# One transformer block's forward and backward on one core: the small vector arithmetic at the turn from forward to backward, regrouped into one set of column sums per norm pair and per gradient pair, with one activation table set

## The chip, the cores and the metric

The kernel runs on one core of one Trainium2 chip. The metric is the device time of one launch in microseconds (us). The kernel before has a median of 1363.42 us in three runs (1362.38 to 1365.44).

## The reference

The reference computes one adaptive-layernorm block on a single token (D = 640, 32 heads of 192, 8192 cached keys and values per head) and its gradients. In the forward,

```
mod = silu(c) @ w_mod                      # sa, ca, ga, sb, cb, gb: six vectors of 640
h   = layernorm(x) * (1 + ca) + sa
x1  = x + ga * attention(h; k_cache, v_cache, wq, wo)
hb  = layernorm(x1) * (1 + cb) + sb
n2  = layernorm(hb)
x2  = x1 + gb * (hb + gelu(n2 @ w3) @ w4)
```

In the reference the mixer's w2 branch reads its hidden vector with shifts by one or two tokens, which for one token gives zeros, so only layernorm, w3, gelu and w4 are left of it. The outputs are x2 and the gradients for x, k_cache, v_cache, wq, wo, w3, w4, c and w_mod. The gradients of the two caches have the size of the caches (32 x 8192 x 192 in bf16 each), so the kernel reads about 340 MB and writes about 226 MB.

Between attention and its backward stands a purely sequential piece: x1, layernorm 1, layernorm 2, u = n2 @ w3, gelu and its derivative, dn2 = du @ w3 transposed, the gradient of layernorm 2, the gradient of layernorm 1, dao = ga * dx1, and do = dao @ wo transposed for the first heads. Only then can the first gradient of V be written. That piece is called the turn here.

## The kernel before

**The work around the turn.** The forward takes the heads in order, two half-heads of K and V at a time. SyncE's queue (SPq) issues all large transfers in program order. K halves lie in `k_mem`, V halves in `v_mem`; a load waits until the half it overwrites has been used. The backward takes the heads in reverse, HS = 31, 30, ...; for each it multiplies V by dO (`bwd_mult`, L1102), writes dV from ScalarE and VectorE (`bwd_dv`), and writes dK from VectorE (`bwd_dk`, L1148). All stores are on the same SyncE queue (`st2`).

**Order.** `pin_order` (L53) fixes, from the first forward product on, that PE, VectorE (DVE) and ScalarE (ACT) execute their instructions in the order of the program text. So the turn is an order written out by hand: a chain of small column operations on tiles of 128 partitions by 5 elements (640 = 5 x 128, the vector stands in columns), with independent work as filler at chosen points.

**The fillers.**
- `dg_some` (L572): VectorE products of w4 rows with the broadcast gradient, 12 in all, one column of `d_g` each.
- `w3T_pe` (L731) and `w3T_act` (L744): the 60 blocks of w3 are transposed by PE (matmul with the identity) in 15 groups of four, each into half or one PSUM bank (tags a, b, s), and copied out by ScalarE. All 15 have to be there before dn2 = du @ w3 transposed (L915) is done.
- `woT_some` (L749): the same for the 15 blocks of the last head pair's wo, in four groups; the matmuls of L1302 read them.

**The sums.** A sum over 640 elements is a DVE reduction per partition and an fp32 matmul against a constant matrix that leaves the total on all partitions: `col_sums` (ones, L144) and `neg_means` (-1/D, L149). `ln_cols` (L154) does one layernorm: sum, centre, square and sum, ScalarE Sqrt (L166), DVE reciprocal, scale. `ln_bwd_cols` (L174) does one gradient: two sums, then four DVE operations. At the turn both are called twice, one after the other, since layernorm 2 reads the result of layernorm 1 and its gradient feeds the gradient of layernorm 1.

**PSUM tiles that matter.** `kb_ps` is one bank: columns 0:384 collect sums of the forward (`fwd_kvK`, L473) and are copied to `kb_sb` by ScalarE (L762); columns 384:512 are `aux_ps` and hold q, u (L875), dn2 (L915), the do columns (L1302) and others. The tag "c" is another bank, with one buffer in this stage: the softmax row `sm`, the sums and the broadcasts take turns on it.

**Around the last head** (L702 to L764): PE sums head 31's output (`fwd_o_mm`), DVE scales it into `o_col_f` and casts to `o_col_bf` (`fwd_o_last`, L533), PE multiplies the last two head pairs by wo into two column groups (`fwd_ao`, L549), DVE adds both to `ao_c` (L763, L764), then `x1_c` (L862), the two `ln_cols` (L864, L868), u (L872), gelu (L879 to L911), dn2 (L913), the two `ln_bwd_cols` (L934, L938), `dao_bf` (L940), do (L1298), its broadcast `do_pb` (L1304), the first dV (L1306) and its store (L1120).

**Later.** `job_mid` (L1159) runs in the second pass of the backward loop (i = 1) and computes x2 and four of the six modulation gradients from `dhb`, `dx1`, `n1_c` and `hb_c`.

ScalarE functions need their table set: the kernel uses Exp almost everywhere and Sqrt in `ln_cols`; two one-column activations on `warm` (L708, L869) place the set changes at the turn.

Of the kernel before, what the change touches and what calls it, by code (L numbers as in the profile page):

```python
# [8 lines left out]
FP32 = mybir.dt.float32  # L9
BF16 = mybir.dt.bfloat16  # L10
ALU = mybir.AluOpType
# [9 lines left out]
def kernel(  # L21
# [78 lines left out]
    def bank_c(name):  # L100
        return bank("c", CB[0], name)

    ident_bf = const.tile([P, P], BF16, name="ident_bf")
    make_identity(nc, ident_bf)
# [4 lines left out]
    nc.vector.memset(ones_mat_f, 1.0)  # L109
    negd_mat = const.tile([P, P], FP32, name="negd_mat")  # L110
    nc.vector.memset(negd_mat, -1.0 / D)
    hot_bf = const.tile([P, 2 * HQ - 1], BF16, name="hot_bf")
# [7 lines left out]
    nc.vector.memset(eps_c, LN_EPS)  # L120
    warm = const.tile([P, 1], FP32, name="warm")
    mask_lo = const.tile([P, 1], FP32, name="mask_lo")
# [6 lines left out]
    def ccol(n, name, dtype=FP32):  # L129
        return const.tile([P, n], dtype, name=name)  # L130

    def mul(out, a, b):
        nc.vector.tensor_tensor(out=out, in0=a, in1=b, op=ALU.mult)  # L133

    def add(out, a, b):
        nc.vector.tensor_tensor(out=out, in0=a, in1=b, op=ALU.add)
# [4 lines left out]
    def stt(out, in0, scalar, in1, op0, op1):  # L141
        nc.vector.scalar_tensor_tensor(out=out, in0=in0, scalar=scalar, in1=in1, op0=op0, op1=op1)

    def col_sums(parts, n, name):  # L144
        ps = bank_c(name)
        nc.tensor.matmul(ps[:, 0:n], lhsT=ones_mat_f, rhs=parts, start=True, stop=True)
        return ps[:, 0:n]

    def neg_means(parts, n, name):  # L149
        ps = bank_c(name)  # L150
        nc.tensor.matmul(ps[:, 0:n], lhsT=negd_mat, rhs=parts, start=True, stop=True)
        return ps[:, 0:n]

    def ln_cols(x_c, pfx, fill=lambda k: None):  # L154
        s1 = ccol(1, pfx + "_s1")
        nc.vector.reduce_sum(out=s1, in_=x_c, axis=AX.X)
        m_ps = neg_means(s1, 1, pfx + "_m")
        fill(0)
        xc = ccol(NDC, pfx + "_xc")
        add(xc, x_c, m_ps.to_broadcast([P, NDC]))  # L160
        sq = ccol(NDC, pfx + "_sq")
        s2 = ccol(1, pfx + "_s2")
        nc.vector.tensor_tensor_reduce(out=sq, in0=xc, in1=xc, scale=1.0 / D, scalar=0.0, op0=ALU.mult, op1=ALU.add, accum_out=s2)
        v_ps = col_sums(s2, 1, pfx + "_v")
        std = ccol(1, pfx + "_std")
        nc.scalar.activation(out=std, in_=v_ps, func=ACT.Sqrt, bias=eps_c[:, 0:1], scale=1.0)  # L166
        fill(1)
        rstd = ccol(1, pfx + "_rstd")
        nc.vector.reciprocal(out=rstd, in_=std)
        nrm = ccol(NDC, pfx + "_n")  # L170
        nc.vector.tensor_scalar(out=nrm, in0=xc, scalar1=rstd[:, 0:1], scalar2=None, op0=ALU.mult)
        return nrm, rstd

    def ln_bwd_cols(dn, n, rstd, add_to, out, pfx, fill=lambda: None):  # L174
        s = ccol(2, pfx + "_s")
        nc.vector.reduce_sum(out=s[:, 0:1], in_=dn, axis=AX.X)
        jk = ccol(NDC, pfx + "_jk")
        nc.vector.tensor_tensor_reduce(out=jk, in0=dn, in1=n, scale=1.0, scalar=0.0, op0=ALU.mult, op1=ALU.add, accum_out=s[:, 1:2])
        m_ps = neg_means(s, 2, pfx + "_m")
        fill()  # L180
        t = ccol(NDC, pfx + "_t")
        mul(t, n, m_ps[:, 1:2].to_broadcast([P, NDC]))
        add(t, t, dn)
        add(t, t, m_ps[:, 0:1].to_broadcast([P, NDC]))
        stt(out, t, rstd[:, 0:1], add_to, ALU.mult, ALU.add)

# [11 lines left out]
    def dve_copy(out, in_):  # L198
        nc.vector.tensor_copy(out=out, in_=in_)
# [114 lines left out]
    q_out(0, 1)  # L314
    cb1 = ccol(NDC, "cb1")
    nc.vector.tensor_scalar(out=cb1, in0=cb, scalar1=1.0, scalar2=None, op0=ALU.add)
    dbo_c = ccol(NDC, "dbo_c")
    mul(dbo_c, dy_c, gb)
    dbo_bf = ccol(NDC, "dbo_bf", BF16)
    dve_copy(dbo_bf, dbo_c)  # L320
# [207 lines left out]
    def fwd_o_prev(h):  # L528
        _, _, bp, ca_, cb_ = head_split(h)
        mul(o_col_f[:, ca_ : ca_ + 1], MA_all[:, h, DH : DH + 1], rinv_bc[:, h : h + 1])  # L530
        mul(o_col_f[bp : bp + 64, cb_ : cb_ + 1], MB_all[bp : bp + 64, h // 2, DH : DH + 1], rinv_bc[bp : bp + 64, h : h + 1])

    def fwd_o_last(h, st):  # L533
        _, _, bp, ca_, cb_ = head_split(h)
        c0 = 3 * (h // 2)
        sl = slice(bp, bp + 64)
        mul(o_col_f[:, ca_ : ca_ + 1], st["o_ps"][:, 0:1], rinv_bc[:, h : h + 1])
        mul(o_col_f[sl, cb_ : cb_ + 1], st["o_ps"][sl, 1:2], rinv_bc[sl, h : h + 1])
        dve_copy(o_col_bf[:, c0 : c0 + 3], o_col_f[:, c0 : c0 + 3])

# [7 lines left out]

    def fwd_ao(hp, wo, sm, c1=408):  # L549
        c0 = 3 * hp  # L550
        for r in range(NDC):
            for cc in range(3):
                nc.tensor.matmul(sm[:, c1 + r : c1 + r + 1], lhsT=wo[:, cc, r * P : (r + 1) * P], rhs=o_col_bf[:, c0 + cc : c0 + cc + 1], start=(cc == 0), stop=(cc == 2))

# [152 lines left out]
    fwd_keep(hl - 1, st[hl - 1])  # L707
    nc.scalar.activation(out=warm, in_=eps_c, func=ACT.Sqrt)  # L708
    fwd_keepB(hl - 1, st[hl - 1])
    fwd_tot(hl, sl_["sm"])  # L710
    fwd_o_mm(hl, 0, sl_)
    fwd_rinv(hl, sl_["sm"])
    fwd_o_prev(hl - 1)
    dg_some(3)
    fwd_o_mm(hl, 1, sl_)
    fwd_o_last(hl, sl_)
    fwd_ao(HH - 2, st[hl - 2]["wo"], sl_["sm"])
    SB = [1024]
# [40 lines left out]
    woT_next = [0]  # L759
    fwd_ao(HH - 1, sl_["wo"], sl_["sm"], 420)  # L760
    fwd_kvK(hl - 1, 3, st[hl - 1])
    nc.scalar.copy(out=kb_sb, in_=kb_ps[:, 0 : 2 * DH])  # L762
    fwd_ao_add(HH - 2, sl_["sm"])  # L763
    fwd_ao_add(HH - 1, sl_["sm"], 420)  # L764
    fek_cm.__exit__(None, None, None)
# [84 lines left out]

    def ln1_fill(k):
        dg_some(1)
        if k == 1:
            w3T_pe(4)
            w3T_act(4)

    def ln2_fill(k):
        w3T_pe(1 + 2 * k)
        dg_some(k)

    x1_c = ccol(NDC, "x1_c")
    mul(x1_c, ao_c, ga)  # L862
    add(x1_c, x1_c, x0_c)
    n1_c, r1 = ln_cols(x1_c, "ln1", ln1_fill)  # L864
    hb_c = ccol(NDC, "hb_c")
    mul(hb_c, n1_c, cb1)
    add(hb_c, hb_c, sb)
    n2_c, r2 = ln_cols(hb_c, "ln2", ln2_fill)  # L868
    nc.scalar.activation(out=warm, in_=eps_c, func=ACT.Exp)  # L869
    n2_bf = ccol(NDC, "n2_bf", BF16)  # L870
    dve_copy(n2_bf, n2_c)
    u_ps = aux_ps[:, 0:NFC]  # L872
    for f in range(NFC):
        for i in range(NDC):
            nc.tensor.matmul(u_ps[:, f : f + 1], lhsT=w3n(i, f * P, (f + 1) * P), rhs=n2_bf[:, i : i + 1], start=False, stop=(i == NDC - 1), skip_group_check=True)  # L875
# [3 lines left out]
    dg_some(2)  # L879
    w3T_act(4)  # L880
    w3T_pe(6)
    dve_copy(u, u_ps[:, 0:NFC])
# [3 lines left out]
    nc.scalar.activation(out=sg, in_=inner, func=ACT.Exp, scale=-2.0 * GELU_K0)  # L886
    w3T_act(1)
    w3T_pe(1)
    w3T_act(6)
# [5 lines left out]
    nc.vector.reciprocal(out=sg, in_=sg)  # L895
    deriv = ccol(NFC, "deriv")
    stt(deriv, sg, 1.0, tb, ALU.subtract, ALU.mult)
# [8 lines left out]
    dg_some(NFC)  # L906
    du_cols(f_late, NFC)
    g_f = ccol(NFC, "g_f")
    mul(g_f, u, sg)
    g_bf = ccol(NFC, "g_bf", BF16)  # L910
    dve_copy(g_bf, g_f)  # L911
    dn2_ps = aux_ps[:, 16 : 16 + NDC]
    for f in range(NFC):  # L913
# [3 lines left out]
    woT_some(1)  # L917
    dn2 = ccol(NDC, "dn2")
    dve_copy(dn2, dn2_ps[:, 0:NDC])
    mid_ps = {"h2": aux_ps[:, 32 : 32 + NDC]}  # L920
# [5 lines left out]

    def lb2_fill():
        woT_some(2)

    def lb1_fill():  # L930
        woT_some(1)

    dhb = ccol(NDC, "dhb")
    ln_bwd_cols(dn2, n2_c, r2, dbo_c, dhb, "lb2", lb2_fill)  # L934
    dn1 = ccol(NDC, "dn1")
    mul(dn1, dhb, cb1)
    dx1 = ccol(NDC, "dx1")
    ln_bwd_cols(dn1, n1_c, r1, dy_c, dx1, "lb1", lb1_fill)  # L938
    dao_bf = ccol(NDC, "dao_bf", BF16)
    mul(dao_bf, dx1, ga)  # L940
    bwd_pf_dve(HS[0])
# [34 lines left out]
    dof = ccol(NQC, "dof")  # L976
    dof_ps = {}
    r3_all = ccol(NQC, "r3_all")
# [180 lines left out]
    def job_mid():  # L1159
        h2 = ccol(NDC, "h2")  # L1160
        add(h2, hb_c, mid_ps["h2"])
        mul(dmod_c[:, 5 * NDC : 6 * NDC], dy_c, h2)
        mul(h2, h2, gb)
        add(h2, h2, x1_c)
        store_cols(out_0[0, 0], h2, const, st2, "x2")
        mul(dmod_c[:, 2 * NDC : 3 * NDC], dx1, ao_c)
        dve_copy(dmod_c[:, 3 * NDC : 4 * NDC], dhb)
        mul(dmod_c[:, 4 * NDC : 5 * NDC], dhb, n1_c)
# [267 lines left out]
```

## Time and profile before

| | |
|---|---|
| median of three runs | 1363.42 us (1362.38 to 1365.44) |
| profiled execution, its own time | 1362.73 us |
| span of its records | 1360.9 us |
| mean granted TensorE clock | 0.791 |
| busy: PE / DVE / ACT | 870.3 / 1079.7 / 918.1 us |
| moved by DMA | 567.63 MB, mean 417 GB/s |
| HBM read / written | 339.94 / 225.91 MB |

Times in the records are counted from the start of the span. The page divides the span into 40 slices of 34 us; a digit is a busy share in tenths. A line of the timeline gives start, duration, engine, line of the program, operation, output and input tiles, count, and in brackets the idle time before it and what ended it. The chain of waits follows the execution back from its last instruction and lists, in order of time, the piece that each moment hung on.

### The profile page before, as it was taken

How to read it: one execution, taken by the hardware profiler on the slowest of the kernel's cores; microseconds unless marked ns; L12 is line 12 of the kernel's file. 1: busy time of each engine (PE TensorE's matmuls, PEld its weight loads, DVE VectorE, ACT ScalarE, POOL GpSimd, SP SyncE). 2: the span in 40 equal slices, each digit the busy share in tenths (PEclk: the TensorE clock that was granted, in tenths of full speed). 3: DMA queues.
4: the chain of work that ended last, by engine and by line, in shares of the span. 5: the costliest groups of instructions: out<-in, count | busy, mean ns of one | idle time of the engine just before them, and what ended most of it. 6: DMA issues, size and time to landing. Idle time of an engine off the chain costs nothing.

```text
span 1360.9 us, 27631 instructions
## 1 busy us (share of the span) xinstructions
PE 870.3 (64%) x11401; PEld 621.5 (46%) x11404; DVE 1079.7 (79%) x1220; ACT 918.1 (67%) x2564; POOL 3.2 (0%) x10
## 2 busy tenths in 40 slices
PE   3698999999999999757666754443333442242422
PEld 3576777777777777746545631111121111010100
DVE  3488888888888887899988987877668978786875
ACT  1387788778788886877766966765467745666570
POOL 0000000000000000000000000000000000000000
PEclk9799999999999999576676666677666776676666
DMA  9999999999999999799999999999999999999997
GB/s 392 417 424 427 426 411 426 419 413 426 422 419 416 424 421 406 270 396 422 422 424 428 427 431 431 431 426 429 427 432 430 433 421 432 425 434 428 429 435 330
DMA packets 46090, 567.63 MB, mean 417 GB/s; under 512 B 4620, under 2 KB 6924, under 8 KB 19084
## 3 DMA queue, kind: packets, MB, share of 16 engines
q1 hardware_dynamic: 45934, 565.86, 98.7%
q8 instruction: 89, 1.46, 0.4%
q14 instruction: 37, 0.30, 0.1%
q10 hardware_dynamic: 30, 0.00, 0.0%
HBM read 339.94 MB, written 225.91 MB: 416 GB/s over the span
## 4 chain that ended last, share of the span: by engine, by line
DMA 45%; PE 18%; DVE 15%; ACT 6%; issue 2%; DVEq 0%; SPq 0%; ACTq 0%
DMA out_dram<-k_mem 24%; DMA v_mem<-in_A_v_cache_dram 17%; DVE k_mem L1093 7%; PE ps_a L456 6%; ACT k_mem L1117 6%; PE ps_b L467 3%; DVE v_mem L133 2%; PE dP_ps L1112 2%; DMA W_sb<-in_w_mod_dram 2%; PE S_ps L396 2%; PE kb_ps L473 1%; DMA k_mem<-in_A_k_cache_dram 1%; DVE prod L133 1%; DVE k_mem L133 1%; PE t_ps L741 0%
## 5 line engine op out<-in xcount | busy, mean ns | idle before, releaser
L1117 ACT ACTIVATE k_mem<-do_pb,PF 128x192 bf16<-128x192 bf16 x1086 | 378.7, 440 | 124.3 <-DMA out_dram<-k_mem 105.0
L1112 PE MATMUL dP_ps<-v_mem,ident_bf 128*128 128x512 bf16 (+2 forms) x960 | 217.5, 400 | 259.6 <-DVE v_mem L133 259.6
L431 ACT ACTIVATE EK<-k_mem,E_f 128x192 bf16<-128x192 bf16 x992 | 354.5, 442 | 37.3 <-issue 20.2
L1112 PEld LDWEIGHTS <-ident_bf 128*128 128x128 bf16 x1056 | 118.8, 118 | 375.6 <-DVE v_mem L133 208.8
L1093 DVE TENSOR_TENSOR k_mem<-dS,q_pb 128x6144 bf16<-128x6144 bf16 x62 | 205.4, 3353 | 50.4 <-DMA out_dram<-k_mem 50.1
L133 DVE TENSOR_TENSOR v_mem<-v_mem,do_pb 128x6144 bf16<-128x6144 bf16 (+1 forms) x62 | 199.1, 3248 | 32.9 <-DMA v_mem<-in_A_v_cache_dram 32.9
L133 DVE TENSOR_TENSOR prod<-k_mem,q_pb 128x6144 bf16<-128x6144 bf16 x62 | 207.6, 3348 | 5.0 <-DMA k_mem<-in_A_k_cache_dram 3.7
L456 PE MATMUL ps_a<-EK,v_mem 128*128 128x193 bf16 x1984 | 191.5, 248 | 16.7 <-DMA v_mem<-in_A_v_cache_dram 14.8
L456 PEld LDWEIGHTS <-v_mem 128*128 128x128 bf16 x1984 | 163.7, 98 | 35.1 <-DMA v_mem<-in_A_v_cache_dram 20.4
L438 DVE TENSOR_TENSOR EK<-k_mem,P2h 128x1536 bf16<-128x1536 bf16 x124 | 117.6, 949 | 0.2 <-issue 0.2
L467 PE MATMUL ps_b<-EK,v_mem 128*64 128x193 bf16 x1984 | 106.8, 249 | 0.0
L396 PE MATMUL S_ps<-prod,ident_bf 64*64 64x256 bf16 x2976 | 95.8, 275 | 7.4 <-DVE prod L133 7.3
L396 PEld LDWEIGHTS <-ident_bf 64*64 64x64 bf16 x3072 | 84.8, 110 | 26.7 <-issue 24.4
L467 PEld LDWEIGHTS <-v_mem 128*64 128x64 bf16 x1984 | 79.9, 109 | 19.1 <-issue 15.5
L1093 DVE TENSOR_TENSOR k_mem<-P2h,do_pb 128x2304 bf16<-128x2304 bf16 (+2 forms) x56 | 74.4, 1358 | 8.4 <-DMA out_dram<-k_mem 7.6
L196 ACT CAST do_pb<-bc_ps 128x384 bf16<-128x384 f32 x15 | 7.1, 471 | 92.7 <-PE bc_ps L192 92.7
L473 PE MATMUL kb_ps<-EK,hot_bf 128*32 128x384 bf16 x992 | 63.5, 333 | 0.0
L1218 PEld LDWEIGHTS <-ident_bf 128*128 128x128 bf16 x100 | 12.5, 125 | 82.7 <-issue 78.5
L436 DVE CAST EK<-E_f 128x16 bf16<-128x16 f32 x124 | 24.2, 195 | 32.5 <-ACT EK L431 22.7
L417 ACT ACTIVATE E_f<-sm_ps,negm 128x64 f32<-128x64 f32 x31 | 9.7, 313 | 57.7 <-DVE negm L415 57.7
L400 DVE TENSOR_REDUCE S<-S_ps 128x128 f32<-128x1024 f32 x32 | 39.2, 1224 | 11.0 <-PE S_ps L396 10.8
L1117 ACT ACTIVATE xt<-do_pb,PF 128x192 bf16<-128x192 bf16 x120 | 41.8, 439 | 0.1
(289 smaller groups left out, 841.3 us busy)
## 6 DMA issues: line engine op xcount, KB each, us to landing
v_mem<-in_A_v_cache_dram SPq DMA_DIRECT2D x47, 3072.0 KB, 18.6
out_dram<-k_mem SPq DMA_DIRECT2D x41, 3072.0 KB, 27.8
k_mem<-in_A_k_cache_dram SPq DMA_DIRECT2D x20, 3072.0 KB, 14.8
out_dram<-k_mem SPq DMA_DIRECT2D x33, 1536.0 KB, 17.8
v_mem<-in_A_v_cache_dram SPq DMA_DIRECT2D x26, 1536.0 KB, 18.6
k_mem<-in_A_k_cache_dram SPq DMA_DIRECT2D x24, 1536.0 KB, 20.6
out_dram<-xt SPq DMA_DIRECT2D x3, 3072.0 KB, 26.2
wq<-in_A_wq_dram SPq DMA_DIRECT2D x3, 2560.0 KB
```

The source lines that it names most:

```text
L133: nc.vector.tensor_tensor(out=out, in0=a, in1=b, op=ALU.mult)
L396: nc.tensor.matmul(st["S_ps"][c0 : c0 + 64, r, t * JH : (t + 1) * JH, :], lhsT=ident_bf[64 * r : 64 * r + 64, 64 * r : 64 * r + 64], rhs=p ...
L400: nc.vector.reduce_sum(out=st["S2"], in_=st["S_ps"], axis=AX.X)
L431: nc.scalar.activation(out=st["EK"][q][:, jj, 0:DH], in_=K_st[h, t][:, r * JQ + jj, :], func=ACT.Copy, scale=st["E_f"][:, j : j + 1])
L436: nc.vector.tensor_copy(out=EK[:, :, DH : DH + 1], in_=st["E_f"][:, q * JQ : (q + 1) * JQ, None])
L438: nc.vector.tensor_tensor(out=EK[:, NA:JQ, 0:DH].rearrange("p j (d r) -> p j d r", r=2), in0=K_st[h, t][:, r * JQ + NA : (r + 1) * JQ, :]. ...
L456: nc.tensor.matmul(st["A_ps"][:, 0:n], lhsT=V_sb[:, r * JQ + jj, a0:a1], rhs=EK[:, jj, 0:n], start=(q == 0 and jj == 0), stop=(q == 3 and ...
L467: nc.tensor.matmul(st["B_ps"][g : g + 64, 0:n], lhsT=V_sb[:, r * JQ + jj, b0:b1], rhs=EK[:, jj, 0:n], start=(q == 0 and jj < 2), stop=(q = ...
L473: nc.tensor.matmul(kb_ps[g : g + 32, 0 : 2 * DH], lhsT=hot_bf[:, HQ - 1 - h : 2 * HQ - 1 - h], rhs=EK[:, jj : jj + 2, 0:DH], start=(h == 0 ...
L1093: nc.vector.tensor_tensor(out=o.rearrange("p j (d r) -> p j d r", r=2), in0=pairs[:, :, None, :].to_broadcast([P, n, NP2, 2]), in1=vec.rea ...
L1112: nc.tensor.matmul(bst[h]["dP_ps"][:, t * JH + r : t * JH + r + n, :], lhsT=ident_bf, rhs=V_sb[:, :, k * w : (k + 1) * w], start=(k == 0), ...
L1117: nc.scalar.activation(out=o[:, jj, :], in_=vec_of(do_pb, h), func=ACT.Copy, scale=bst[h]["PF"][:, t * JH + jj : t * JH + jj + 1])
```

## The change

1. **Tables.** One set that holds both exponential and logarithm is loaded at the start. The inverse root is exp(-0.5 ln(v/D + eps)) on ScalarE (two activations), in place of Sqrt and a DVE reciprocal; the two `warm` activations go.
2. **Both norms from one sum.** Moments of sb (its centred form `sbc`, its variance) and products with 1 + cb are computed in the setup. At the turn, the mean of x1 comes from two one-column matmuls into one PSUM column (one of them with a partial x1 that is ready early); then one DVE operation forms three products of the centred x1, one squares two of them, and one matmul sums 20 columns. From the four sums come both inverse roots, `n1_c` and `n2_bf`.
3. **Last head.** `fwd_o_last` writes the bf16 columns first and the fp32 columns after; both last `fwd_ao` accumulate into one column group.
4. **Both gradients from one sum.** Before dn2 is known, 30 columns are summed and turned into the coefficients of a linear map (`lnb_sums`: three DVE operations and one matmul; `lnb_map1` and `lnb_map2`: three and seven DVE operations). With dn2 come four products, one matmul of 20 columns, and `dao_bf` as a sum of five terms (`lnb_dao`). The full `dhb` and `dx1` are computed in `job_mid` (`lnb_rest`, eleven DVE operations; x2 takes two more there, since hb is formed anew).
5. **Fillers and the `kb_sb` copy** are placed anew: five groups of w3T transposes stand before u and ten after it (eight and seven before); the copy of `kb_sb` moves from before the norms to after `lnb_dao`, ahead of the do matmuls.

The core of the diff:

```diff
+    nc.scalar.preload_act_table_set("natural_log_exp_and_others")
...
-        nc.scalar.activation(out=std, in_=v_ps, func=ACT.Sqrt, bias=eps_c[:, 0:1], scale=1.0)
+    def rsqrt_col(out, in_, scale, bias):
+        nc.scalar.activation(out=out, in_=in_, func=ACT.Ln, bias=bias, scale=scale)
+        nc.scalar.activation(out=out, in_=out, func=ACT.Exp, scale=-0.5)
+
+    def rows_sum(out, ps):
+        nc.vector.reduce_sum(out=out, in_=ps.rearrange("p (k i) -> p k i", i=NDC), axis=AX.X)
...
+    nc.vector.reduce_sum(out=sbs, in_=sb, axis=AX.X)
+    sb_ps = col_sums(sbs, 1, "sb_m")
+    stt(sbc, sb_ps.to_broadcast([P, NDC]), -1.0 / D, sb, ALU.mult, ALU.add)
...
+    sb_ps = col_sums(sbv, 1, "sb_v")
...
+        dve_copy(o_col_bf[:, ca_ : ca_ + 1], o_col_f[:, ca_ : ca_ + 1])
+        dve_copy(o_col_bf[bp : bp + 64, cb_ : cb_ + 1], o_col_f[bp : bp + 64, cb_ : cb_ + 1])
...
-        mul(o_col_f[:, ca_ : ca_ + 1], st["o_ps"][:, 0:1], rinv_bc[:, h : h + 1])
-        mul(o_col_f[sl, cb_ : cb_ + 1], st["o_ps"][sl, 1:2], rinv_bc[sl, h : h + 1])
-        dve_copy(o_col_bf[:, c0 : c0 + 3], o_col_f[:, c0 : c0 + 3])
+        for o in (o_col_bf, o_col_f):
+            mul(o[:, ca_ : ca_ + 1], st["o_ps"][:, 0:1], rinv_bc[:, h : h + 1])
+            mul(o[sl, cb_ : cb_ + 1], st["o_ps"][sl, 1:2], rinv_bc[sl, h : h + 1])
...
-    nc.scalar.activation(out=warm, in_=eps_c, func=ACT.Sqrt)
...
+    mul(xp, ao_c, ga)
+    add(xp, xp, x0_c)
+    nc.vector.tensor_tensor_reduce(out=T5[:, 0, :], in0=xp, in1=ZW[:, 0, :], scale=-1.0 / D, scalar=0.0, op0=ALU.mult, op1=ALU.add, accum_out=sxp)
     fwd_rinv(hl, sl_["sm"])
...
-    fwd_ao(HH - 1, sl_["wo"], sl_["sm"], 420)
+    fwd_ao(HH - 1, sl_["wo"], sl_["sm"], 408, False)
     fwd_kvK(hl - 1, 3, st[hl - 1])
-    nc.scalar.copy(out=kb_sb, in_=kb_ps[:, 0 : 2 * DH])
-    fwd_ao_add(HH - 2, sl_["sm"])
-    fwd_ao_add(HH - 1, sl_["sm"], 420)
...
+    def fill0():
+        dg_some(1)
+
+    def fill1():
+        dg_some(1)
+        w3T_pe(4)
+
+    def fill2():
+        w3T_pe(1)
+
+    def fill3():
+        w3T_act(3)
...
+    mean_mm(sxp)
+    nc.vector.tensor_tensor_reduce(out=hc, in0=ao_ps, in1=ga, scale=-1.0 / D, scalar=0.0, op0=ALU.mult, op1=ALU.add, accum_out=s_t)
+    mean_mm(s_t)
+    stt(x1_c, hc, -float(D), xp, ALU.mult, ALU.add)
+    add(ao_c, ao_c, ao_ps)
+    FILL[0]()
+    stt(T5[:, 0:3, :], bc3(x1_c, 3), m_ps, ZW[:, 0:7:3, :], ALU.add, ALU.mult)
+    mul(T5[:, 3:5, :], T5[:, 0:3:2, :], T5[:, 0:3:2, :])
+    ln_ps = col_sums(T5[:, 1:5, :].rearrange("p k i -> p (k i)"), 4 * NDC, "ln_s")
+    FILL[1]()
+    rows_sum(S4, ln_ps)
+    rsqrt_col(r1, S4[:, 2:3], 1.0 / D, eps_c[:, 0:1])
+    nc.vector.tensor_scalar(out=nsa, in0=S4[:, 1:2], scalar1=-1.0 / D, scalar2=None, op0=ALU.mult)
+    stt(va, S4[:, 1:2], nsa, S4[:, 3:4], ALU.mult, ALU.add)
+    nc.vector.tensor_scalar(out=hc, in0=T5[:, 2, :], scalar1=nsa, scalar2=None, op0=ALU.add)
+    FILL[2]()
+    stt(vt, va, r1, S4[:, 0:1], ALU.mult, ALU.add)
+    nc.vector.tensor_scalar(out=vt, in0=vt, scalar1=r1, scalar2=ndvsb, op0=ALU.mult, op1=ALU.max)
+    rsqrt_col(r2, vt, 1.0 / D, eps2)
+    stt(hc, hc, r1, sbc, ALU.mult, ALU.add)
+    nc.vector.tensor_scalar(out=n1_c, in0=T5[:, 0, :], scalar1=r1, scalar2=None, op0=ALU.mult)
+    nc.vector.tensor_scalar(out=n2_bf, in0=hc, scalar1=r2, scalar2=None, op0=ALU.mult)
+    FILL[3]()
...
     dg_some(2)
-    w3T_act(4)
-    w3T_pe(6)
+    lnb_sums()
+    w3T_pe(4)
+    w3T_act(2)
     dve_copy(u, u_ps[:, 0:NFC])
...
-    w3T_act(1)
-    w3T_pe(1)
+    w3T_act(4)
+    w3T_pe(6)
     w3T_act(6)
...
     du_cols(f_late, NFC)
+    lnb_map1()
+    lnb_map2()
...
+    def lnb_dao():
+        dn2 = dn2_ps[:, 0:NDC]
+        mul(T5[:, 1:5, :], ZW[:, 0:10:3, :], bc3(dn2, 4))
+        ps = col_sums(T5[:, 1:5, :].rearrange("p k i -> p (k i)"), 4 * NDC, "lb_s")
+        woT_some(2)
+        mul(base, G1, dn2)
+        add(base, base, X5[:, 0, :])
+        rows_sum(S4, ps)
+        mul(T5[:, 1:5, :], X5[:, 1:5, :], k_bc(S4, 4))
+        nc.vector.reduce_sum(out=G1, in_=T5[:, 1:5, :].rearrange("p k i -> p i k"), axis=AX.X)
+        add(dao_bf, base, G1)
...
-    ln_bwd_cols(dn2, n2_c, r2, dbo_c, dhb, "lb2", lb2_fill)
-    dn1 = ccol(NDC, "dn1")
-    mul(dn1, dhb, cb1)
-    ln_bwd_cols(dn1, n1_c, r1, dy_c, dx1, "lb1", lb1_fill)
-    mul(dao_bf, dx1, ga)
+    lnb_dao()
+    woT_some(1)
+    nc.scalar.copy(out=kb_sb, in_=kb_ps[:, 0 : 2 * DH])
     bwd_pf_dve(HS[0])
...
     def job_mid():
-        add(h2, hb_c, mid_ps["h2"])
+        lnb_rest()
+        mul(h2, n1_c, cb1)
+        add(h2, h2, sb)
+        add(h2, h2, mid_ps["h2"])
```

## The prediction

> **What bounds the kernel now.** I read the page's slices first: where the memory is idle, time can be won.
>
> ```profile
> PEclk9799999999999999576676666677666776676666
> DMA  9999999999999999799999999999999999999997
> GB/s 392 417 424 427 426 411 426 419 413 426 422 419 416 424 421 406 270 396 422 422 424 428 427 431 431 431 426 429 427 432 430 433 421 432 425 434 428 429 435 330
> ```
>
> All slices move about 420 GB/s but one: slice 17 (544 to 578 us), the turn. The kernel is bound by DMA on both sides of it, so a microsecond won or lost in the turn shifts the end by one. The stretches of 5 us show the hole; the last two columns are DMA share and GB/s, the number before them the granted PE clock.
>
> ```profile
> 545.00:550.00 5.00, 4.85 (x42) 4.63 (x43) 3.44 (x16) 3.58 (x7) 0.00 (x0) 0.50 0.85 342
> 550.00:555.00 5.00, 5.00 (x108) 5.00 (x107) 4.18 (x17) 4.99 (x13) 0.00 (x0) 0.50 0.39 162
> 555.00:560.00 5.00, 4.22 (x66) 3.47 (x64) 2.46 (x20) 3.03 (x8) 0.00 (x0) 0.50 0.86 294
> 560.00:565.00 5.00, 4.07 (x90) 3.98 (x90) 3.48 (x8) 3.37 (x11) 0.00 (x0) 0.50 0.18 69
> ```
>
> PE (first number) and ACT (fourth) are nearly full from 550 to 555, at half clock: a change that shortens DVE's chain meets them. So the chain of waits comes next.
>
> ```profile
> 545.61 1.73 PE t_ps L741 x16
> ...
> 548.77 1.30 PE t_ps L741 x12
> 550.08 1.58 PE kb_ps L875 x60
> 551.65 3.01 PE t_ps L741 x28
> 554.66 1.47 PE kb_ps L915 x56
> ...
> 556.94 0.60 PE lb_m L151 x2
> ...
> 559.01 0.57 PE lb_m L151 x2
> ...
> 560.68 0.56 PE kb_ps L1302 x15
> ```
>
> Up to 556.42 the chain hangs mostly on PE: 60 transposes (28 in 3.01 us: 0.1075 us each, 6.45 us), u (1.58), dn2 (1.75). Only behind dn2 is it the small DVE chain: 556.42 to the end of `dao_bf` at 560.63. The timeline gives the rest:
>
> ```profile
> 538.83 1.01 PE L518 MATMUL sm_ps<-E_all,v_mem 128*128 128x1 bf16 x32 [0.27 <-DVE rinv_bc L504]
> 549.09 1.28 ACT L869 ACT_TABLE_LOAD   x1
> 559.95 0.48 ACT L755 CAST wo_t<-t_ps 128x384 bf16<-128x384 f32 x1 [0.85 <-PE t_ps L754]
> 563.36 0.35 SPq L1120 DMA_DIRECT2D out_dram<-dV  x1
> ```
>
> In the first line PE waits until DVE has read other columns of the same bank (400:402 read, 416:418 written): accesses to one bank are put in order. In the last, the first store ends the hole.
>
> **Prices.** A dependent DVE operation on a few columns starts 0.20 us after the one before; with a per-partition scalar 0.26; independent ones 0.08; one that reads PSUM 0.17. An fp32 matmul of one or two columns gives its result after 0.56 to 0.60 and holds PE for 0.45. A product for `d_g` takes 0.75, a copy of four transposed blocks on ACT 0.51 (four in 2.05), a one-column activation 0.26 with a bias tile, 0.21 without.
>
> **Step 1, last head to ao.** Two casts more before the `d_g` products cost 0.19. `fwd_o_last` has four operations that read PSUM instead of two and a cast; by the bank order PE's wo products wait for the fourth: it ends at 542.05, and the 30 matmuls (28 took 0.90) end at 543.04, against 542.82: **+0.22**. Bounds: -0.15 if the first wo products slip in, +0.4 if the 0.16 gap before the 28 stays on top.
>
> **Step 2, ao (T) to the end of dn2.** Now 13.60 us (542.82 to 556.42). After: `fwd_kvK` (0.76 of PE) and two mean matmuls follow on PE, so the mean stands at T+1.75; the first `d_g` product and the sums of DVE lie beside them. Product, square (T+2.2), matmul of 20 columns (no such row; 0.56 for one column and 0.49 for 128 at full clock bound it: 0.62), row sums T+3.15, logarithm and exponential T+3.7 (DVE's `nsa`, `va`, `hc` beside them), `vt` in two operations T+4.25, logarithm and exponential T+4.8, `n2_bf` T+5.07. Now `n2_bf` is ready at T+6.9, and u starts at T+7.26 behind transposes: the norms gain about 2 us. But PE gives it back. Before u it has done five groups, not eight (2.15 us, until T+4.95); u runs T+5.12 to T+6.7; then stands the 30-column matmul, whose inputs wait for two `d_g` products and three operations of DVE (T+7.2): PE idles 0.6 and works 0.5. From T+7.8 come ten groups, 40 x 0.1075 = 4.3, to T+12.1, and dn2, 1.75, to **T+13.85**. ACT beside it: first copies at T+4.8 (behind the second exponential), 15 x 0.51 with the gelu exponential after the fifth, the last at T+13.4: just early enough, no cover left. DVE: gelu and three `d_g` products to T+11.5, maps and `g_bf` to T+13.75: hidden, by 0.1. So **+0.25**. The two table loads that go (1.28 each, at 536.85 and 549.09) were beside idle ACT time and PE's transposes: nothing by themselves. Bounds -0.4 (30-column inputs early) to +1.0 (ACT 0.7 later).
>
> **Step 3, dn2 (end D) to the end of the do matmuls.** Now 4.81 (556.42 to 561.23). After: products D+0.2, PE's first wo group before the sum, sum at D+0.95, then row sums, product, reduction, addition: `dao_bf` at D+1.75 in place of D+4.21. Late next are the wo transposes: groups two and three follow the sum on PE (0.43 each), the fourth waits for a free buffer; their ACT copies end at about D+2.75. Then the moved `kb_sb` copy (0.48 at 543.62 now; 0.45 back to back) reads the bank that the do matmuls write, so these start at D+3.25 and end at **D+3.82**: **-0.99**. Bounds: -2.4 (all hidden but the chain, 4.21 - 1.75) and +0.3.
>
> The Trainium skill, "PSUM — Partial Sum Buffer", section "PSUM bank collisions raise a hardware error", says to guard PSUM by bank and quadrant rather than by address, reads of ScalarE against writes of TensorE included. The 538.83 row agrees. By it the copy stands on the path; by addresses alone the do matmuls would start 0.45 earlier (the third rival).
>
> **Step 4, the start.** The setup gains eight DVE operations and two matmuls on a one-buffer bank, at worst some 4 us before the first product (26.23). The K loads issued around then land after 20.6 to 30.7 us, the V loads after 24.0, against 6.8 for a V half issued at 576.89 into an emptier queue: over 10 us of queue hide it. **0**; if that cover is gone, up to +4. The table load at the start moves ahead of three tiny loads by 1.28; their chain ends at 9.7, and the modulation waits for `w_mod` until 16.27: 0.
>
> **Step 5, job_mid.** Thirteen operations more on a DVE without gaps (5.00 of 5 us): about 2.45 us at 612, all behind it later. Does DMA starve? The dV store issued at 618.77 lands after 8.8 us; half its size landed in 3.3 in the hole, so about 5.2 alone (1.9 more at 0.4 MB per us): 3.6 of queue hide the 2.45. **0**, bounds 0 to +2.45. The queue behind it is SyncE's: the dV stores, then the wo load.
>
> The wo load behind the last w3T transposes is issued 0.7 later than 554.48; it landed in 6.7, by then 561.9, before the first store's bytes. 0.
>
> **Sum.** 0.22 + 0.25 - 0.99 = **-0.5 us** on the profiled execution (1362.73, span 1360.9, 1.8 around it): 1362.2. That execution is 0.7 below the median; against 1363.42 I forecast **1362.9**. A measurement here can tell about 0.2% (2.7 us) from no change: this is no change.
>
> **Rivals.**
> 1. *The chain of small operations binds everywhere.* If PE and ACT keep up (the order on them is less tight than I laid it), the norms give 1.85, the gradients 4.21 - 1.75 = 2.46, less 0.22: -4.1, **1359.3**. For: two sums are gone from each half. Against: PE full from 550 to 555. 0.13.
> 2. *Slower: the sets alternate.* If the loaded set isn't kept, logarithm and exponential each bring a load: four times 1.28, all on the path before u (PE has only its five groups to do meanwhile, done at T+4.95), 5.1 us on top of the forecast: **1368.0**. It decides from the first logarithm after an exponential. Against: the present trace shows loads only where the function changes sets, with copies running under either. 0.06. This is also the case in which the change doesn't do what it says. The Trainium skill ("ScalarE: Activation LUTs", "What ACT_TABLE_LOAD costs") gives 1283 ns and a drain of 1380 for a switch; the row at 549.09 agrees with the first, and the next activation starts at 550.38, without the second. By the page the four would cost 10.6.
> 3. *Bank order doesn't hold the do matmuls*: 0.45 less, **1362.4**. Against: the 538.83 row. 0.08.
> 4. *job_mid isn't hidden*: the store queue is too short (the DMA share is 0.71 in the stretch 612 to 613): +2.45, **1365.3**. 0.09.
>
> **Numbers.** Forecast 0.64, rivals 0.13, 0.06, 0.08, 0.09. Faster by over 0.2% (below 1360.7) only rival 1: 0.13. Slower by over 0.2% (above 1366.1) only rival 2: 0.06. Within: 0.81. Range 1360.0 to 1365.6: the bounds of steps 1 to 3 (-2.95 to +1.7) rarely meet at one end, and rival 4 lies inside; it leaves out rivals 1 and 2, 0.19.
>
> **What would show it.** After: one table load; `n2_bf` some 5 us behind ao and u nearly 2 us sooner than now; 40 transposes without a break before L915, its end again near 557; `dao_bf` under 2 us behind dn2, and PE waiting for ACT before L1302; job_mid some 2.5 us longer with DMA full beside it. Wrong if PE reaches dn2 before 555.5, if L1302 follows `dao_bf` at once, or if the first store moves by over 1.5 us.

## The result, and the profile after

The changed kernel takes **1365.63 us** (median; 1364.79 to 1366.70), the kernel before beside it on the same chip 1362.56 (1361.52 to 1365.44): ratio **1.0023**, 95% interval 1.0016 to 1.0030. It is 3.07 us slower; 0.5 us faster was forecast (1362.9, range 1360.0 to 1365.6). The profiled execution took 1365.14, its span is 1363.1.

The page's slices of the changed kernel (the same three rows, 34.1 us a slice):

```profile
PEclk9699999999999998566676676676666767666666
DMA  9999999999999999699999999999999999999997
GB/s 391 417 425 428 427 414 424 423 411 426 423 421 414 424 423 405 256 401 392 424 425 427 428 427 433 430 428 430 428 427 433 424 427 432 426 435 428 432 431 335
```

The hole has become deeper, 256 GB/s for 270, and a second shallow one stands two slices behind it (392 for 422, at 613 to 648 us). So I looked in two places. The stretches of the turn (DMA share and GB/s last):

```profile
545.00:550.00 5.00, 4.53 (x83) 4.31 (x84) 4.40 (x21) 3.05 (x8) 0.00 (x0) 0.50 0.78 321
550.00:555.00 5.00, 3.56 (x32) 3.40 (x33) 3.63 (x15) 3.22 (x7) 0.00 (x0) 0.50 0.33 136
555.00:560.00 5.00, 4.75 (x89) 4.50 (x87) 3.14 (x21) 4.12 (x9) 0.00 (x0) 0.50 0.51 166
560.00:565.00 5.00, 3.73 (x90) 3.48 (x88) 2.09 (x4) 3.43 (x11) 0.00 (x0) 0.50 0.36 142
```

From 550 to 555, where PE and ACT were full before, they are now busy 3.56 and 3.22 of 5 us: neither is short of work, they wait for each other. The chain of waits says where (start, length, what):

```profile
547.40 0.23 DVE n_bf L918
...
549.81 0.60 PE lz_s L144 x2
550.41 0.44 PE t_ps L757 x4
550.88 0.59 ACT w3T_t L762
551.46 0.11 ACT sg L993
551.57 1.95 ACT w3T_t L762 x4
553.56 2.72 PE t_ps L757 x24
556.28 1.62 PE kb_ps L1023 x60
...
560.88 0.39 ACT kb_sb L1035
561.32 0.55 PE kb_ps L1399 x15
```

and the timeline gives the idle time ahead of each in brackets, with what ended it:

```profile
0.74 1.28 ACT L103 ACT_TABLE_LOAD   x1 [0.74 <-PEq L1517]
...
550.88 0.59 ACT L762 CAST w3T_t<-t_ps 128x512 bf16<-128x512 f32 x1 [1.43 <-PE t_ps L757]
...
553.56 2.72 PE L757 MATMUL t_ps<-ident_bf,k_mem 128*128 128x128 bf16 x24 [1.44 <-ACT w3T_t L762]
...
561.32 0.54 PE L1399 MATMUL kb_ps<-dao_bf,wo_t 128*128 128x1 bf16 x15 [0.95 <-ACT kb_sb L1035]
...
564.06 1.21 SPq L1214 DMA_DIRECT2D out_dram<-dV  x2
```

Ao ends at T = 542.55. n2_bf starts at T+4.85 (547.40) and is there at T+5.08, 1.84 us sooner than before, but dn2 ends at 557.91, **T+15.36**, for T+13.60 before. ScalarE's copy of group 4 waits 1.43 us, though that group had been transposed before u (PE's twenty transposes there end at 547.60); the gelu exponential stands behind it; then PE's group 9 waits 1.44 us for the copy of group 8. Behind dn2 it is nearly as forecast: do ends 3.96 us later (3.82 forecast, 4.81 before).

The second place is job_mid. Stretches of the changed kernel (first fence), and of the kernel before:

```profile
626.00:627.00 1.00, 1.00 (x12) 0.90 (x10) 0.67 (x3) 0.00 (x0) 0.00 (x0) 1.00 0.33 135
627.00:628.00 1.00, 0.89 (x16) 0.74 (x13) 0.07 (x1) 0.00 (x0) 0.00 (x0) 1.00 1.19 504
...
630.00:632.00 2.00, 2.00 (x13) 1.91 (x13) 2.00 (x1) 1.97 (x5) 0.00 (x0) 0.59 0.81 217
```

```profile
626.00:628.00 2.00, 1.81 (x13) 1.73 (x13) 1.93 (x4) 2.00 (x5) 0.00 (x0) 0.85 1.03 436
...
630.00:632.00 2.00, 2.00 (x11) 1.93 (x11) 2.00 (x2) 2.00 (x7) 0.00 (x0) 0.50 1.02 416
```

Against some 425 GB/s the first stretch of the changed kernel loses 0.7 us of transfer and the last 1.0, the middle one gives 0.2 back. Before, the stretches of 2 us from 622 to 632 all lie between 399 and 457 GB/s. The same SyncE issues in both traces say it once more: the changed kernel's is 0.49 early at the last load before the turn, 0.70 late at the first dV store, 0.19 late at 611, 2.88 late at 624, behind job_mid, and 2.56 late at the last.

### The profile page after: what moved, and what is told of

The parts are those of the page before. It is cut to its first block, busy times and chain, and to the rows that moved or that the text cites. A ratio compares the mean times of both kernels' runs of the same rounds, so it can differ in the third digit from the quotient of the medians.

```text
span 1363.1 us, 27659 instructions
## 1 busy us (share of the span) xinstructions
PE 868.4 (64%) x11403; PEld 621.3 (46%) x11406; DVE 1083.4 (79%) x1247; ACT 914.1 (67%) x2561; POOL 3.2 (0%) x10
## 3 DMA queue, kind: packets, MB, share of 16 engines
q8 instruction: 89, 1.46, 0.4%
## 4 chain that ended last, share of the span: by engine, by line
DMA 32%; DVE 17%; PE 12%; ACT 7%; issue 2%; DVEq 0%; SPq 0%; ACTq 0%
DMA out_dram<-k_mem 20%; DMA v_mem<-in_A_v_cache_dram 8%; DVE k_mem L1187 8%; ACT k_mem L1211 5%; PE dP_ps L1206 4%; DVE v_mem L131 3%; DMA k_mem<-in_A_k_cache_dram 3%; DMA W_sb<-in_w_mod_dram 2%; PE ps_a L467 2%; PE ps_b L478 1%; DVE prod L131 1%; PE S_ps L407 1%; DVE V_sb L131 1%; PE kb_ps L484 1%; ACT EK L442 1%
```

## The experiments

Each stands beside runs of the kernel before on the same chip. The table gives the difference of the medians and the ratio with its interval; these intervals reach about 1.2 us to either side (0.95 in the first measurement), so a smaller difference isn't told from none.

| kernel | us to before | ratio (95%) |
|---|---|---|
| changed, first and second time (e13) | +3.07, +2.76 | 1.0023 (1.0016-1.0030), 1.0023 (1.0014-1.0032) |
| e1 job_mid late | +1.61 | 1.0013 (1.0004-1.0022) |
| e2 pairs whole by order | +1.36 | 1.0012 (1.0003-1.0021) |
| e3 both | -0.48 | 0.9999 (0.9990-1.0008) |
| e4 before, with idle operations | +1.94 | 1.0014 (1.0005-1.0022) |
| e5 e3, kb_sb late | -1.14 | 0.9994 (0.9985-1.0002) |
| e6 e5, sums late | -0.41 | 0.9995 (0.9986-1.0004) |
| e7 before, one table | +0.59 | 1.0004 (0.9995-1.0013) |
| e8 before, job_mid late | +0.28 | 1.0001 (0.9992-1.0009) |
| e9 e5, DVE's order | -1.56 | 0.9989 (0.9980-0.9998) |
| e10 pairs shifted, first and second time (e14) | +3.32, +1.91 | 1.0020 (1.0011-1.0028), 1.0017 (1.0008-1.0026) |
| e11 e9, one copy early | -1.29 | 0.9990 (0.9981-0.9999) |
| e12 pairs shifted, job_mid late | -1.03 | 0.9992 (0.9983-1.0001) |

My theory after the traces: the 3 us are two things, the split of tile pairs at the turn (1.4) and job_mid (some 2). Rivals: the new order as such is too slow; or job_mid is hidden and all is the turn.

### job_mid: e1, e4, e8

e1 moves job_mid in the changed kernel, e8 makes the same edit in the kernel before, and e4 adds thirteen operations to the head of job_mid in the kernel before, of which no output comes:

```diff
         if i == 1:
             mid_cols()
+        if i == 7:
             job_mid()
...
```

> The changed kernel with one edit: the x2 and modulation job (with the gradient operations that the change moved into it) runs in the eighth pass of the backward loop (i = 7) instead of the second (i = 1). Theory A (the 13 added vector operations, 2.7 us, fall into a stage where VectorE has no gaps and the store queue is short, and cost 2.0 us of the 3.07 us): 1363.6, that is 2.0 below the changed kernel, and the first store of the turn unmoved. Theory B (all of the loss is in the turn, and the queue would have hidden the job): 1365.6. Theory C (the job costs its full 2.7 us and more, since also its old part moves to a free place): 1362.9 or less.

> The kernel before with 13 dependent vector operations on 5 columns, whose result nothing uses, put ahead of the x2 job in the second pass of the backward loop (2.6 us of VectorE). Theory A (the place itself has no cover): 2.0 us above the kernel before, 1364.5. Theory B (3.6 us of queued stores hide 2.6 us, as the prediction had it): 1362.5, no change.

```diff
+        mul(pad, x1_c, x1_c)
+        for k in range(12):
+            add(pad, pad, x1_c)
```

> The kernel before with nothing changed but job_mid moved from the second to the eighth pass of the backward loop. Theory (the place had just enough queued stores for the old job_mid; only the thirteen added operations starve the queue): the same time as the kernel before, within 0.3 us. Rival (job_mid already cost something there): 0.5 to 1.5 us faster than the kernel before; then the 0.5 us that the changed kernel with both repairs is below the kernel before would be the place of job_mid and not the regrouped sums.

All three came out by the theory, e1 with a smaller gain than the 2.0 expected: it keeps the turn as it is and is 1.46 lower against before than the changed kernel (1.6 by the spans). In its stretches the hole is gone:

```profile
626.00:628.00 2.00, 2.00 (x13) 1.91 (x13) 2.00 (x1) 1.97 (x6) 0.00 (x0) 0.63 1.00 424
...
630.00:632.00 2.00, 2.00 (x10) 1.94 (x10) 2.00 (x4) 2.00 (x7) 0.00 (x0) 0.50 0.98 401
```

e4 puts 2.6 us of operations that nobody needs in the same place of the kernel before and pays 1.94: the place has too little cover, whatever the operations are. In e8 the old job_mid costs nothing there that can be told (+0.28), so moving it is no gain of its own.

### The tile pairs: e2, e3, e10, e12 to e14

A group fills 512 columns, one bank. The transposes of groups (2,3), (4,5), (8,9), (10,11) lie in the two halves of one PSUM tile of 1024 columns, two banks. The changed order does five groups, u, four groups, six groups: it cuts 4|5 and 8|9. e2 keeps pairs together by another order:

```diff
     def fill2():
-        w3T_pe(1)
+        w3T_pe(2)
...
-    w3T_pe(4)
-    w3T_act(2)
+    w3T_pe(2)
+    w3T_act(3)
...
-    w3T_act(4)
+    w3T_act(2)
     w3T_pe(6)
+    w3T_act(1)
+    w3T_pe(1)
     w3T_act(6)
```

> The changed kernel with one edit: the groups of transposed w3 blocks that share one two-bank PSUM tile (4 with 5, 8 with 9) are no longer separated by a copy of one of them; six groups before u, then 2, 6 and 1. Theory A (ScalarE's copy of group 4 waits for group 5 to be written into the other half of its tile, and PE's group 9 waits for the copy of group 8; 1.43 us of idle ACT and 1.44 us of idle PE): dn2 ends about 1.4 us sooner behind ao, about 13.9 us instead of 15.4, and the time falls by 1.4 to 1364.2. Theory B (PE and ACT are slow there for want of work and the order of groups does not matter): no gap closes, 1365.6.

> Both edits of the two runs before together. Theory A (two independent causes): 3.4 us below the changed kernel, 1362.2, within 0.5 of the kernel before. If the two losses overlap (a later first store only uses up idle time that the job would use as well), only about 2 us are won: 1363.6.

Both by theory: in e2 dn2 ends at T+13.45 and the first store is 1.74 us early instead of 0.70 late (part of that is the granted clock, which was up from 554 to 557 in this execution); with both edits (e3) the slowdown is gone. But e2 moves instructions too. e10 moves none: it only lets the pairs begin at another group.

```diff
-            if b in (2, 4):
+            if b in (1, 3):
...
-            elif b < 2:
-                w3T_ps[g] = bank("ab"[b], name="t_ps")
+            elif b in (0, 5):
+                w3T_ps[g] = bank("ab"[b == 5], name="t_ps")
```

> The changed kernel with one edit: the w3T groups that share a two-bank PSUM tile are (1,2), (3,4), (7,8), (9,10), (13,14) and not (2,3), (4,5), (8,9), (10,11), (14). Every instruction stands where it stood, in the same number; only the tiles differ, and no pair is split by the order any more. Theory (a copy out of one half of a tile waits for the transposes into the other half, and the other way round): both waits of 1.4 us, the copy of group 4 and the transposes of group 9, are gone, dn2 ends 1.2 to 1.9 us sooner behind ao, and the time is that of the kernel with whole pairs by order, 1.1 to 1.9 us above the kernel before. Rival (the order itself makes PE and ScalarE late, the tiles have no part in it): no gain, 3.1 us above the kernel before.

In time the rival seemed to have it (+3.32), in the trace the theory: the five copies and the forty transposes run without a break, and dn2 ends at T+13.94. Nor can the two waits of the changed kernel have been waits for a free buffer: group 4 had been transposed long before its copy, and group 8 stood in the tile of group 9 already. So I measured it again beside the changed kernel, and with job_mid moved.

> The changed kernel with the w3T pairs shifted by one, measured a second time, now beside the changed kernel on the same chip. Theory (the gain at the turn reaches the end): 1.5 to 2.1 us above the kernel before. Rival (it is lost behind job_mid): 2.8 to 3.4 above.

> The changed kernel itself, beside the shifted one on the same chip. By the first measurement 3.1 us above the kernel before. If the shifted pairs are worth their 1.4 us at the turn, the shifted kernel is 1.0 to 1.6 below this one; if they are worth nothing, the two agree within 0.5.

> The changed kernel with the w3T pairs shifted by one (order unchanged) and job_mid in the eighth pass instead of the second. Theory (the turn's gain is real and is lost again only behind job_mid, where VectorE's thirteen operations meet a store queue that is too short): 0.4 us below to 0.3 us above the kernel before, as with whole pairs by order and late job_mid (0.5 below). Rival (the waits at the tiles were not what the turn cost): as the changed kernel with late job_mid alone, 1.6 us above the kernel before.

Timeline of e14, in which the last head ends 0.04 us after that of e13:

```profile
547.43 2.54 ACT L762 CAST w3T_t<-t_ps 128x512 bf16<-128x512 f32 x5
...
550.26 4.45 PE L757 MATMUL t_ps<-ident_bf,k_mem 128*128 128x128 bf16 x40
...
562.68 1.21 SPq L1214 DMA_DIRECT2D out_dram<-dV  x2
```

Neither 1.4 us wait is left, and the first store is issued at 562.68 for 564.05 in e13: **1.37 us** for a choice of tiles. Measured, the difference is 0.85 (1.91 against 2.76; 1.0 to 1.6 was expected). With job_mid late (e12 against e1) it is 2.6, more than the turn's own gain, and e12 comes out lower than expected. Each of these four figures carries an interval of about 1.2 us to either side, and e10 by itself shows no gain, so the mechanism is shown and the sum is not settled. Where part of it goes is seen behind the turn, in the 48 matmuls that the next V load waits for, e13 first, then e14:

```profile
572.75 4.40 PE L1206 MATMUL dP_ps<-v_mem,ident_bf 128*128 128x128 bf16 x48 [4.81 <-DVE v_mem L131]
577.18 0.34 SPq L355 DMA_DIRECT2D v_mem<-in_A_v_cache_dram  x1
```

```profile
571.38 5.28 PE L1206 MATMUL dP_ps<-v_mem,ident_bf 128*128 128x128 bf16 x48 [4.81 <-DVE v_mem L131]
576.69 0.34 SPq L355 DMA_DIRECT2D v_mem<-in_A_v_cache_dram  x1
```

They start 1.37 sooner and the load only 0.49, since they take 0.88 longer: in both kernels the granted clock is 0.50 until 576 and 0.97 and 0.69 in the microsecond from there. By these shares it rose about half a microsecond later in e14, so part of the loss belongs to this execution and not to the tiles.

### Tables alone: e7

```diff
+    nc.scalar.preload_act_table_set("natural_log_exp_and_others")
...
-        nc.scalar.activation(out=std, in_=v_ps, func=ACT.Sqrt, bias=eps_c[:, 0:1], scale=1.0)
...
-        nc.vector.reciprocal(out=rstd, in_=std)
+        nc.scalar.activation(out=rstd, in_=v_ps, func=ACT.Ln, bias=eps_c[:, 0:1], scale=1.0)
+        nc.scalar.activation(out=rstd, in_=rstd, func=ACT.Exp, scale=-0.5)
```

> The kernel before with the tables alone: one set for exponential and logarithm loaded at the start, exp(-0.5 ln) in the place of Sqrt and reciprocal, no activations on warm. Theory (both loads stood beside idle time or beside PE's transposes): the same time as the kernel before, within 0.3 us, and one table load in the trace. Rival (the load of 1.28 us in front of the ScalarE copies at 549.09 was on the path of the w3T copies): 0.5 to 1.3 us faster. Other rival (the sets alternate): four loads or more, over 2 us slower.

One load in its trace, at 0.73, and +0.59, more than the 0.3 expected but with an interval that includes no change: no gain from the tables alone can be seen, and they don't alternate.

### What the regrouping can give: e5, e6, e9, e11

e5 is e3 with the copy of `kb_sb` behind the do matmuls:

```diff
-    nc.scalar.copy(out=kb_sb, in_=kb_ps[:, 0 : 2 * DH])
...
     dve_copy(do_bf[:, 3 * PS[0] : 3 * PS[0] + 3], do_ps[:, 0:3])
+    nc.scalar.copy(out=kb_sb, in_=kb_ps[:, 0 : 2 * DH])
```

> The changed kernel with the w3T pairs kept whole and job_mid in the eighth pass, and in addition the copy of kb_sb moved behind the copy of the first do columns, out of the way of the do matmuls. Theory (the copy holds the do matmuls because PSUM accesses to one bank are put in order): the do matmuls start when dao_bf is there or when the last wo copy is out, 0.40 to 0.45 us sooner behind dn2 than with the copy ahead of them, and the time is 0.4 below that of the kernel with the pairs and the late job_mid (which was 0.5 below the kernel before), so about 0.9 us below the kernel before. Rival (the last wo copy on ScalarE holds them anyway, the copy only sits behind it): no gain, 0.5 us below the kernel before.

```profile
558.30 0.51 PE L1400 MATMUL kb_ps<-dao_bf,wo_t 128*128 128x1 bf16 x12
...
559.08 0.24 PE L1400 MATMUL kb_ps<-dao_bf,wo_t 128*128 128x1 bf16 x3 [0.27 <-ACT wo_t L771]
```

Twelve of the fifteen no longer wait, and the last three wait only for their wo copy. From the end of that copy to the end of do it is 0.29 us, for 0.99 in the changed kernel. The time, 0.66 lower against before than e3, agrees but is inside the interval.

e6 moves `lnb_sums` behind the last transposes as well.

```diff
-    lnb_sums()
     w3T_pe(2)
...
     w3T_pe(1)
+    lnb_sums()
     w3T_act(6)
```

> As the kernel with kb_sb late, and in addition the 30-column sums (three DVE operations and one fp32 matmul) moved behind the exponential of gelu and the last w3T transposes of PE. Theory A (PE from the end of u to the end of dn2 is the bound, and the sums cost it their 0.45 us and an idle 0.2 to 0.6 us): dn2 ends 0.6 to 1.0 us sooner and the time is 1.5 to 1.9 us below the kernel before. Theory B (DVE's gelu chain with its filler products ends last by then): the maps now come later on DVE, dn2 ends at the same moment, and the time stays 0.9 below the kernel before.

Theory B: the products of dn2 start at T+13.85, T+13.44 in e5, since DVE's row of d_g products and maps now ends last; PE's sum behind them has waited for DVE (dn2 itself ends at T+12.78, for T+13.45 in e3, in part at a higher granted clock):

```profile
557.30 0.40 PE L144 MATMUL lb_s<-T,ones_mat_f 128*128 128x20 f32 x2 [1.05 <-DVE T L131]
```

So e9 leaves the sums in place and shortens DVE's row ahead of the products; the lines of `g_f` and `g_bf` go behind `lnb_dao` too.

```diff
     def lnb_map2():
...
-        mul(X3, X3, bc3(X5[:, 3, :], 3))
-        nc.vector.tensor_scalar(out=X5[:, 1:5, :], in0=X5[:, 1:5, :], scalar1=r2, scalar2=-1.0 / D, op0=ALU.mult, op1=ALU.mult)
-        add(X5[:, 0, :], X5[:, 0, :], gady)
...
     def lnb_dao():
...
         mul(base, G1, dn2)
+        X3 = X5[:, 0:3, :]
+        mul(X3, X3, bc3(X5[:, 3, :], 3))
+        nc.vector.tensor_scalar(out=X5[:, 1:5, :], in0=X5[:, 1:5, :], scalar1=r2, scalar2=-1.0 / D, op0=ALU.mult, op1=ALU.mult)
+        add(X5[:, 0, :], X5[:, 0, :], gady)
```

> The kernel with the whole pairs, the late job_mid and the late kb_sb copy, and in addition two edits of VectorE's order: g_f and g_bf behind the chain to dao_bf, and the last three operations of the map behind the four products of dn2, under PE's sum. In the kernel without these edits dn2 ends at 555.38 and the products start at 556.09, behind DVE's own queue. Theory (DVE is what comes last at dn2 since PE and ScalarE have been repaired): the products start 0.5 to 0.65 us sooner, and the time is 1.5 to 1.8 us below the kernel before. Rival (the wo copies of ScalarE hold the do matmuls anyway): 1.1 below, as without the edits.

```profile
556.00 0.18 DVE L131 TENSOR_TENSOR T<-ZW,kb_ps 128x20 f32<-128x20 f32 x1 [0.79 <-PE kb_ps L1022]
...
557.69 0.98 PE L1401 MATMUL kb_ps<-dao_bf,wo_t 128*128 128x1 bf16 x15
...
560.80 1.21 SPq L1216 DMA_DIRECT2D out_dram<-dV  x2
```

The time is as expected, the reason only half: DVE now waits for PE, but the products start at T+13.49, no sooner, because the transposes ran at half clock here (36 in 4.03 us; in e5 32 of them took 1.95). The gain lies behind dn2: do ends 2.72 us after it, 3.94 in e5. e9 is the version that **beats both kernels**: 0.9989 (0.9980 to 0.9998) of the kernel before, 1.6 us below it and 4.6 below the changed one, each taken against its own runs of before. The interval only just leaves out no change, and e9 is the lowest of several versions; e11, which contains its edits, agrees (0.9990, 0.9981 to 0.9999).

e11 adds one w3T copy in the idle 0.60 us of ScalarE between the two norms.

```diff
     def fill2():
+        w3T_act(1)
         w3T_pe(2)
```

> As the kernel with both edits of VectorE's order, and in addition the first w3T copy of ScalarE in the 0.60 us in which ScalarE is idle between the exponential of r1 and the logarithm of r2. Theory (ScalarE's row of fifteen copies sets the end of dn2, on which PE waits 0.58 and 0.24 us in the kernel without): a further 0.3 to 0.5 us, 1.9 to 2.3 us below the kernel before. Rival (the copy, 0.51, delays the logarithm by as much as it saves, or DVE's last du columns come last): no further gain, 1.5 to 1.8 below.

No further gain. The copy fits (546.19 to 546.77, the logarithm starts at once), but ScalarE has then caught up with the others: it waits 0.46 us for DVE's `inner` ahead of the gelu exponential, where e9 doesn't wait, and behind it for PE, 0.41 us where it was 0.35:

```profile
550.80 1.07 ACT L762 CAST w3T_t<-t_ps 128x512 bf16<-128x512 f32 x2 [0.41 <-PE t_ps L757]
```

## Why the prediction was wrong

**Step 1** was right: +0.22, from rinv to ao 4.43 us for 4.21.

**Step 2 failed**, at "From T+7.8 come ten groups, 40 x 0.1075 = 4.3, to T+12.1". The ten groups start at T+7.68 (7.8 forecast), but not in one row: I had given every group a place of its own. In a pair that the order cuts, the copy out of one half waits for the transposes into the other, and the other way round. The term was +1.76, not +0.25. With shifted pairs, the case I had worked out, dn2 ends at T+13.94 to T+13.96 in e10, e12 and e14 (13.85 forecast). I had read "accesses to one bank are put in order" into the wait at 538.83; there, bank and tile are the same. The two halves here are different banks of one tile, and wait 1.43 and 1.44 us: what is put in order is the tile. The Trainium skill ("PSUM — Partial Sum Buffer", "PSUM bank collisions raise a hardware error") asks for a guard by bank and quadrant. By that rule the halves would be free and step 2 would have ended near T+13.9; the waits measured go beyond it. Whether a guard by bank alone would do here wasn't tried.

**Step 3** was right in its mechanism and nearly in size: -0.85, forecast -0.99, with `dao_bf` 1.74 us behind dn2 (1.75), and PE waiting for ACT before the do matmuls. The shortfall is 0.14. Rival 3 is out; e5 shows that the copy did hold them.

**Step 4** was right: one table load at 0.74, first product at 26.51 (26.23 before), no load late because of it.

**Step 5 failed**, at "3.6 of queue hide the 2.45". Thirteen operations took 2.69 us, and e1 and e4 price such a delay at 1.5 and 1.9 (each with an interval of over 1 us). The 3.6 us were the queue in front of one store. That store was indeed covered; but everything behind job_mid comes 2.69 late, the next stores too, and the one at 626 found the queue nearly empty (DMA share 0.33 in 626 to 627). I should have taken the thinnest queue among all issues that follow, not the first. This is rival 4, which had 0.09 and the price 2.45.

**The sum**: with +1.51 for step 2, +0.14 for step 3 and 1.5 to 1.9 for step 5, the forecast of -0.52 becomes +2.6 to +3.1; measured were +3.07 and +2.76. That the time lies only just above the range is no credit to it: the upper end was reached by two errors, of which the sum held neither. The signs named for a wrong forecast didn't appear (PE came to dn2 at 556.08, the do matmuls waited for ScalarE, the first store moved by 0.70); two of those named for a right one failed, the 40 transposes without a break and the full DMA beside job_mid. Rival 1 didn't come, nor would it have without the tile waits: PE's transposes and ScalarE's copies still set the end of dn2 (T+13.4 to T+13.5 in e2 and e9, T+12.7 in e5, where the granted clock was up). Rival 2 didn't come: the set stays loaded.

## What to carry to other kernels

Before work is redistributed between engines by hand, list which pieces share a tile: here an order that cut a shared tile made both engines wait 1.4 us, although each row looked free. Work that is moved out of a critical stretch is free only where the thinnest transfer queue behind its new place covers it; try it with idle operations in that place first. And a gain in the middle of a kernel is worth only what is left of it after the next stage with a limit of its own.

## What the hardware showed beyond that

The granted TensorE clock steps on a grid of its own. In the stretches of one microsecond it leaves 0.50 behind the turn between 573.8 and 577 in every kernel here, for 6.8 us, while the first store lies between 560.8 and 564.1; in some executions it also is up inside the turn, for about 3.4 or 6.8 us (554 to 557 in e2, 548 to 555 in e5), in others not (before, changed, e14). In eight of the nine traces with both rises these lie 20.5 us apart, six times 3.41, and in e5 27.3, eight times, though the work between them differs. The grid lies otherwise against the launch in each execution, and the first store scatters by no less than the rise, so these traces don't tell whether work moved by a microsecond or two can move the rise by a whole step. The Trainium skill ("TensorE: Matmul & The Clock Gate", "The HAM clock gate (the "warmup" mystery)") describes a window of about 3.4 us that runs free of the kernel; the lengths agree. It also lets the clock rise after one busy window; here PE was busy 5.00 of 5 us at 550 to 555 in e14 and 3.49 of 3.50 from 552.7 to 556.2, one step of its grid, at 0.50 there and in the 3.4 us behind, so that part isn't borne out. A gain ahead of such a step can shrink, as 1.37 us did to 0.49 in e14.
